# Attention and two gated MLPs on one core: the second pass's products with w_in, w_gate and w_val by a Strassen scheme

## The chip, the cores and the metric

The kernel runs on one core of one Trainium2 chip. The metric is the device time of one execution in microseconds, the median of three runs. PE (TensorE) multiplies, DVE (VectorE), ACT (ScalarE) and POOL (GpSimd) work elementwise, and all transfers are issued from the queue of SP (SyncE).

## What is computed

```python
scores = cap * np.tanh(scale * q @ k^T / cap)        # batch 4, 12 heads, 448 tokens, head size 64
attn   = softmax(scores) @ v                         # -> x, 1792 tokens x 768
x = np.maximum(x @ w_in, 0) ** 2 @ w_out             # 768 -> 2048 -> 768
y = (sigmoid(x @ w_gate) * (x @ w_val)) @ w_out2     # 768 -> 1536 -> 768
```

The weights come as 64-bit floats.

## The kernel before

The tokens are worked off in two passes. The first pass has 768 tokens, as column blocks of 256 and 512; the second has 1024, as two blocks of 512. Each pass runs both MLPs. Attention comes first and then runs interleaved with the first pass, since x of the second pass is needed late. The feature dimension of 768 is six tiles of 128 (`CC`); the hidden layers are 16 and 12 tiles, taken in groups of four (`FG`).

Every float32 product is made of three: each operand is split into a rounded high half (`hi`, by ACT) and the rest (`lo = x - hi`, by DVE for activations, by POOL for weights), and `products` adds lo·hi, hi·lo and hi·hi into one PSUM bank (lines 540 to 542). A unit is one such product: with w_in, w_gate or w_val it has 6 x 3 matmuls (`unit_a`), with an output matrix 4 x 3 (`unit_b`). Four banks, tag `pn`, go round; a bank is free again when its result has been taken out: by ACT for the relu (`relu`) and the sigmoid (`gate`), by DVE for the gate's product (`val`, line 585) and for the additions into `acc` (`total`, line 603). After that the hidden values are split again (`split_g`, tiles `gx`).

In the first pass each weight tile is converted from 64 bits on DVE (lines 498 to 504, tile `raw`), kept in DRAM in 32 bits, split (`round_w`, tiles `wh` and `wl`, four of each) and used; the second pass loads the 32-bit copy and splits it again. x of the second pass is split as soon as it is ready, stored to DRAM (`xn`, `store_x`), and loaded again once attention is through (`load_x`), into tiles `xa` in memory that attention has left. Between the passes the pool `mlp0` is closed and `mlp1` opened in its place (`turn_over`).

The order of each engine's instructions is written when the program is built: `Flow` plays the jobs off against costs per operation (lines 131 to 150), each engine takes what is ready by rank and age, and `pick` gives PE the next unit or attention step. On the chip each engine then works in that fixed order and waits on semaphores.

## Time and profile before

| | |
|---|---|
| median of 3 runs | 1204.4 us (1204.39 to 1205.56) |
| span of the profiled execution | 1206.0 us |
| PE busy | 1182.8 us (98%), 5880 matmuls |
| DVE, ACT, POOL busy | 661.7 (55%), 583.5 (48%), 277.0 us (23%) |
| mean granted TensorE clock | 0.995 |

The profiled execution has no time of its own beside its span, so the span stands for it; it is 1.6 us above the median of the runs. Busy time of PE counts matmuls from their start to their modelled end, so overlapping ones fill it up. All times of an engine are from the trace of this one execution.

### The profile page before, as it was taken

Reading aid. Unit: us, or ns where it says so; the run is one execution under the profiler, and the core shown is the slowest. Engines: PE = TensorE matmul, PEld = TensorE weight load, DVE = VectorE, ACT = ScalarE, POOL = GpSimd, SP = SyncE. Lnnn points to the kernel's source line nnn. Section 1 sums busy time; section 2 is a strip of 40 time slices with the busy share of each in tenths; the row PEclk is TensorE's granted clock in tenths of the full one; section 3 lists DMA queues with packets and bytes.
Section 4 is the critical chain, followed back from the end, with each engine's and each line's share of the span. In section 5 each row is a group of like instructions: output and inputs, shape, how many; then the busy total and the mean of one; then the engine's idle time right before and its main releaser. Section 6 shows DMA issues by size and latency. Waiting matters only on the chain.

```text
span 1206.0 us, 15410 instructions
## 1 busy us (share of the span) xinstructions
PE 1182.8 (98%) x5880; PEld 968.0 (80%) x5880; DVE 661.7 (55%) x943; ACT 583.5 (48%) x862; POOL 277.0 (23%) x174
## 2 busy tenths in 40 slices
PE   7999999998999989999999999999999999999998
PEld 4556788887888878888888888888888888888887
DVE  3699789888989988889972102212153210221222
ACT  7876567574677677765533434251432223221220
POOL 0021222322212223222322221312122123123110
PEclk9999999999999999999999999999999999999999
DMA  4565666555645656555686111211121112112112
GB/s 161 151 196 153 183 195 181 189 170 164 187 143 175 191 164 211 179 184 176 177 287 228 40 58 35 70 28 60 45 61 53 35 44 66 40 40 66 44 44 96
DMA packets 70490, 149.81 MB, mean 124 GB/s; under 512 B 20497, under 2 KB 28945, under 8 KB 70417
## 3 DMA queue, kind: packets, MB, share of 16 engines
q1 hardware_dynamic: 70416, 148.84, 40.0%
q8 instruction: 46, 0.75, 0.2%
q14 instruction: 28, 0.22, 0.1%
HBM read 110.10 MB, written 38.62 MB: 123 GB/s over the span
## 4 chain that ended last, share of the span: by engine, by line
PE 80%; DVE 11%; DMA 3%; ACT 3%; issue 2%; SPq 0%; POOL 0%; DVEq 0%; ACTq 0%; POOLq 0%
PE pn L540 24%; PE pn L541 24%; PE pn L542 24%; PE pv L365 6%; PE se L321 2%; DVE raw L502 2%; DVE raw L504 1%; DVE raw L500 1%; ACT pt L212 1%; DVE raw L498 1%; DVE pt L408 1%; DVE pt L215 1%; DMA sg<-pt 1%; DMA s_wv<-raw 1%; DMA w<-in_w_dram 1%
## 5 line engine op out<-in xcount | busy, mean ns | idle before, releaser
L525 POOL TENSOR_TENSOR wl<-raw,wh 128x512 fp32r<-128x512 f32 (+1 forms) x164 | 274.0, 1671 | 897.5 <-ACT wh L212 739.7
L540 PE MATMUL pn<-xa,wl 128*128 128x512 f32 (+1 forms) x960 | 350.2, 365 | 0.0
L541 PE MATMUL pn<-xa,wh 128*128 128x512 f32 (+1 forms) x960 | 349.6, 364 | 0.0
L542 PE MATMUL pn<-xa,wh 128*128 128x512 f32 (+1 forms) x960 | 349.1, 364 | 0.0
L212 ACT ACTIVATE wh<-raw 128x512 fp32r<-128x512 f32 (+1 forms) x160 | 117.2, 732 | 313.1 <-PE pn L542 259.8
L541 PE MATMUL pn<-gx,wh 128*128 128x512 f32 (+1 forms) x672 | 244.3, 364 | 3.9 <-DVE gx L215 3.9
L540 PE MATMUL pn<-gx,wl 128*128 128x512 f32 (+1 forms) x672 | 244.6, 364 | 0.0
L542 PE MATMUL pn<-gx,wh 128*128 128x512 f32 (+1 forms) x672 | 244.0, 363 | 0.0
L540 PEld LDWEIGHTS pn<-xa,wl 128*128 128x128 f32 x960 | 182.1, 190 | 31.2 <-issue 3.0
L542 PEld LDWEIGHTS pn<-xa,wh 128*128 128x128 f32 x960 | 182.1, 190 | 28.5
L541 PEld LDWEIGHTS pn<-xa,wh 128*128 128x128 f32 x960 | 182.0, 190 | 27.9
L215 DVE TENSOR_TENSOR gx<-g,gx 128x512 fp32r<-128x512 f32 (+1 forms) x112 | 87.1, 778 | 161.4 <-ACT gx L212 160.9
L541 PEld LDWEIGHTS pn<-gx,wh 128*128 128x128 f32 x672 | 127.1, 189 | 23.6 <-DVE gx L215 4.3
L603 DVE TENSOR_TENSOR acc<-pn,acc 128x512 f32<-128x512 f32 (+1 forms) x120 | 74.3, 621 | 127.4 <-PE pn L542 126.8
L540 PEld LDWEIGHTS pn<-gx,wl 128*128 128x128 f32 x672 | 127.0, 189 | 21.4 <-issue 1.9
L542 PEld LDWEIGHTS pn<-gx,wh 128*128 128x128 f32 x672 | 127.1, 189 | 19.8
L585 DVE TENSOR_TENSOR g<-pn,r 128x512 f32<-128x512 f32 (+1 forms) x48 | 29.7, 620 | 169.7 <-PE pn L542 169.7
L365 PE MATMUL pv<-pt,v 128*128 128x448 f32 x360 | 112.7, 447 | 5.2 <-DVE pt L218 1.9
L365 PEld LDWEIGHTS pv<-pt,v 128*128 128x128 f32 x360 | 64.6, 189 | 39.5 <-issue 23.0
L212 ACT ACTIVATE gx<-g 128x512 fp32r<-128x512 f32 (+1 forms) x112 | 64.5, 576 | 64.6 <-DVE g L585 62.6
L212 ACT ACTIVATE r<-pn 128x512 f32<-128x512 f32 (+1 forms) x112 | 59.8, 534 | 66.8 <-PE pn L542 66.7
L212 ACT ACTIVATE raw<-w 128x512 f32<-128x512 f32 (+1 forms) x78 | 60.9, 781 | 57.3 <-DMA s_w<-raw 21.1
(71 smaller groups left out, 1044.8 us busy)
## 6 DMA issues: line engine op xcount, KB each, us to landing
w<-in_w_dram SPq DMA_DIRECT2D x16, 768.0 KB
w<-in_w_dram SPq DMA_DIRECT2D x24, 512.0 KB
w<-in_wg_dram SPq DMA_DIRECT2D x12, 768.0 KB
w<-in_wv_dram SPq DMA_DIRECT2D x12, 768.0 KB
w<-in_wo_dram SPq DMA_DIRECT2D x18, 512.0 KB
s_w<-raw SPq DMA_DIRECT2D x16, 384.0 KB
s_w<-raw SPq DMA_DIRECT2D x24, 256.0 KB
xa<-xn SPq DMA_DIRECT2D x12, 512.0 KB
```

What stands on the lines that cost most here:

```text
L212: return on("ACT", flow.act(cols(out)) + extra, lambda: nc.scalar.activation(out=out, in_=in_, func=func, **kw), rank)
L215: return on("DVE", flow.dve(cols(out)), lambda: nc.vector.tensor_tensor(out=out, in0=a, in1=b, op=ALU.subtract), rank)
L321: nc.tensor.matmul(out=sc[:, x, :S], lhsT=w[r, c0:c0 + P], rhs=a[r, :S], start=i == 0, stop=i == 2)
L365: nc.tensor.matmul(out=o[:, j, :S], lhsT=w, rhs=pt[r, u], start=step == 0 and m == 0, stop=step == 3 and m == len(terms) - 1)
L408: yield on("DVE", flow.dve(S), lambda: nc.vector.tensor_tensor(out=xu[r], in0=xe[r, j], in1=bc[r], op=ALU.mult), 0 if early(n) else 2)
L502: yield on("DVE", flow.dve(n), lambda: nc.vector.scalar_tensor_tensor(out=mu, in0=lo, scalar=29, in1=mu, op0=ALU.logical_shift_right, op1= ...
L525: yield on("POOL", 0.15 + n * 0.0023, lambda: nc.gpsimd.tensor_tensor(out=lo, in0=raw, in1=f32(hi), op=ALU.subtract))
L540: nc.tensor.matmul(out=o, lhsT=wl[:, s], rhs=hi, start=i == 0, stop=False)
L541: nc.tensor.matmul(out=o, lhsT=wh[:, s], rhs=lo, start=False, stop=False)
L542: nc.tensor.matmul(out=o, lhsT=wh[:, s], rhs=hi, start=False, stop=i == n - 1)
L585: yield on("DVE", flow.dvep(w), lambda: nc.vector.tensor_tensor(out=g, in0=o, in1=st["r", k, f, off], op=ALU.mult))
L603: yield on("DVE", flow.dvep(w), lambda: nc.vector.tensor_tensor(out=acc, in0=o, in1=acc, op=ALU.add))
```

## The change

Only the second pass changes its products with w_in, w_gate and w_val. Two hidden tiles of 128 (f and f + 2) by two blocks of 512 tokens are one group: the weights are blocks a11, a12, a21, a22 (hidden tile by half of the six feature tiles), the activations b11, b12, b21, b22 (half of the feature tiles by token block). Four outputs took eight block products of 3 x 3 matmuls; now seven take their place, numbered 1 to 7:

- sums of weights, DVE, 384 columns each: s1 = a21 + a22, s2 = s1 - a11, s3 = a11 - a21, s4 = a12 - s2
- differences of activations, DVE, 512 columns each: t1 = b12 - b11, t2 = b22 - t1, t4 = t2 - b21, t3 = b22 - b12
- products: 1 = a11·b11, 2 = a12·b21, 3 = s4·b22, 4 = a22·t4, 5 = s1·t1, 6 = s2·t2, 7 = s3·t3
- PE takes them as 1, 2, 6, 4, 7, 5, then product 1 of the next group, then 3. Products 1, 6 and 7 are added up in one bank, each copied out by ACT between (`cp`); 5 and 3 share another bank. DVE makes the outputs: 2 + cp1, 4 subtracted from cp7, 5 + cp7 and 3 + cp6.

All sums are of float32 before the split into high and low halves, which now is made for 7 x 3 activation tiles (before 6 of double width) and, per group, for 7 weight halves of 384 columns. There are 8 groups for w_in and 12 for w_gate and w_val.

Around it: x of the second pass is stored unsplit (half the bytes), loaded in 12 pieces of 256 KB and combined (`combine`); for the second MLP `second` combines the sums of w_out. Four more banks, tag `pq`, take the place that attention's banks leave. The closing products with w_out and the last matrix start with the hidden tiles of the first group (units of 6 matmuls, `part`). The weights of the second pass go through the two `w64` tiles. Early q and k tiles use the buffers of `gx`.

```diff
-WSTART, ATT, XGAP, SLACK = 5, 0.82, 2.0, 1.0
+WSTART, ATT, SLACK = 5, 0.82, 1.0
+R1, G1, CP, TM = 8, 3, 5, 3
+HK = CC // 2
+RANK = {"x": 1, "y": 0}
+FORM = {"1": "b11", "2": "b21", "6": "t2", "4": "t4", "7": "t3", "5": "t1", "3": "b22"}
...
+    def after_attention():
+        close_pool("att")
+        close_pool("ps")
+        open_pool("act1", "right")
...
+        open_pool("units1", "left", space=bass.MemoryType.PSUM)
...
+    def split(kind, name, i, src, temp=None):
...
+        yield act(dst[:, 0], src, rank=RANK[kind])
+        yield sub(dst[:, 1], src, f32(dst[:, 0]), RANK[kind])
...
+    def combine(kind, i, raw, event):
...
+        yield sub(t1, raw["b12"], raw["b11"], RANK[kind])
...
+        yield sub(t2, raw["b22"], t1, RANK[kind])
...
+        yield sub(t4, t2, raw["b21"], RANK[kind])
...
+        yield sub(t3, raw["b22"], raw["b12"], RANK[kind])
...
+    def weight_sums(grp, raw):
...
+        yield add2(s1, a21, a22)
+        yield sub(s2, s1, a11)
...
+        yield sub(s3, a11, a21)
+        yield sub(s4, a12, s2)
...
+    def low(m, h, hi, lo, src, res, item):
+        n = cols(src)
+        yield on("POOL", 0.15 + n * 0.0023, lambda: nc.gpsimd.tensor_tensor(out=lo, in0=src, in1=f32(hi), op=ALU.subtract))
...
+    def strassen(u, kind, gi, j, num):
+        grp = kind, gi, j
+        m, h = u["m"], u["half"]
+        slot = ("bank", grp, {"1": "b", "6": "b", "7": "b", "2": "a", "4": "d", "5": "e", "3": "e"}[num])
...
+        o = products(m, HK, lambda i: st[src, FORM[num], i], 0, SP, st[slot], h * HW, first=bool(u["bank"]))
+        return shares(grp, num, o)
+
+    def shares(grp, num, o):
...
+        if num in "167":
+            yield "take", "cp"
+            t = st["cp", grp, num] = T("mlp1", "cp", [P, SP], bufs=CP)
+            yield act(t, o, rank=0)
...
+        part = {"2": "1", "4": "7", "5": "7", "3": "6"}[num]
+        yield "until", ("cp", grp, part)
+        yield "take", "r1"
+        c = T("mlp1", "r", [P, SP], bufs=R1)
+        yield post(c, o, st["cp", grp, part], ALU.subtract if num == "4" else ALU.add)
...
+        needs += {"6": [("cp", grp, "1")], "7": [("cp", grp, "6")], "3": [("sum", grp, "5")]}.get(num, [])
...
+                    for num in "126475":
+                        add_s(kind, gi, j, num)
+                        if held and num == "1":
+                            add_s(*held, "3")
```

Where the instructions move, on DVE: the end of the first pass, from the low half of the last hidden tile (`gx`) on; `acc` rows give PE its banks back, `raw` rows convert weights. Before:

```order
L215 TENSOR_TENSOR gx<-g,gx 128x512
L498 TENSOR_SCALAR raw<-raw 128x512
L603 TENSOR_TENSOR acc<-pn,acc 128x256
L500 TENSOR_SCALAR raw<-raw 128x512
L502 SCALAR_TENSOR_TENSOR raw<-w_6281,raw 128x512
L504 SCALAR_TENSOR_TENSOR raw<-w_6281,raw 128x512
L603 TENSOR_TENSOR acc<-pn,acc 128x512 x2
```

Changed, from the same row on (`tm` is a difference, `xa` a low half):

```order
L220 TENSOR_TENSOR gx<-g,gx 128x512
L220 TENSOR_TENSOR xa<-tm,xa 128x512
L822 TENSOR_TENSOR acc<-pn,acc 128x256
L220 TENSOR_TENSOR tm<-tm,xa 128x512
L647 TENSOR_SCALAR raw<-raw 128x512
L649 TENSOR_SCALAR raw<-raw 128x512
L822 TENSOR_TENSOR acc<-pn,acc 128x256
L220 TENSOR_TENSOR xa<-xa 128x512
L220 TENSOR_TENSOR xa<-tm,xa 128x512
L220 TENSOR_TENSOR tm<-xa,tm 128x512
```

Rows of the second pass's x now stand between the additions.

On DVE, the end of the second pass's products with w_out. Before, additions and low halves alternate:

```order
L603 TENSOR_TENSOR acc<-pn,acc 128x512
L215 TENSOR_TENSOR xa<-acc,xa 128x512
L603 TENSOR_TENSOR acc<-pn,acc 128x512
L215 TENSOR_TENSOR xa<-acc,xa 128x512
L603 TENSOR_TENSOR acc<-pn,acc 128x512
L215 TENSOR_TENSOR xa<-acc,xa 128x512
L585 TENSOR_TENSOR g<-pn,r 128x512
```

Changed, up to the addition for product 2 of the first w_gate group (`r<-cp,pq`):

```order
L822 TENSOR_TENSOR acc<-pq,acc 128x512
L822 TENSOR_TENSOR acc<-pn,acc 128x512
L822 TENSOR_TENSOR acc<-pq,acc 128x512
L220 TENSOR_TENSOR tm<-acc 128x512
L220 TENSOR_TENSOR xa<-acc,xa 128x512
L220 TENSOR_TENSOR tm<-acc,tm 128x512
L220 TENSOR_TENSOR xa<-acc,xa 128x512
L220 TENSOR_TENSOR xa<-tm,xa 128x512
L220 TENSOR_TENSOR tm<-tm,acc 128x512
L220 TENSOR_TENSOR xa<-tm,xa 128x512
L226 TENSOR_TENSOR r<-cp,pq 128x512
```

The last three additions now come in one piece, and seven rows of the last operands follow.

On PE, the first group of w_in, from the last matmul of product 2 to the first of product 4, with what each row waits for:

```order
L698 MATMUL pq<-xa,wh 128x512
L695 MATMUL pn<-xa,wl 128x512 [waits Activation_49,Pool_49]
L697 MATMUL pn<-xa,wh 128x512
L698 MATMUL pn<-xa,wh 128x512
L695 MATMUL pn<-xa,wl 128x512
L697 MATMUL pn<-xa,wh 128x512
L698 MATMUL pn<-xa,wh 128x512
L695 MATMUL pn<-xa,wl 128x512
L697 MATMUL pn<-xa,wh 128x512
L698 MATMUL pn<-xa,wh 128x512
L695 MATMUL pq<-xa,wl 128x512 [waits Pool_49]
```

Before, a unit was 18 such rows in a bank of its own; product 6 here goes on in the bank of product 1, behind ACT's copy.

## Rows read from the trace of the kernel before

**Rows 1.** The page: busy us, share of the span and instructions of each engine.
```profile
PE 1182.8 (98%) x5880; PEld 968.0 (80%) x5880; DVE 661.7 (55%) x943; ACT 583.5 (48%) x862; POOL 277.0 (23%) x174
```

**Rows 2.** Windows: length, busy us of PE, PEld, DVE, ACT, POOL, clock, DMA, GB/s.
```profile
648.00:1200.00 552.00, 552.00 (x2437) 457.24 (x2436) 119.27 (x152) 163.54 (x259) 122.49 (x79) 1.00 0.17 52
600.00:650.00 50.00, 50.00 (x281) 43.88 (x280) 29.51 (x47) 15.19 (x25) 14.75 (x11) 1.00 0.89 311
```

**Rows 3.** Timeline: start, us, engine, line; 256 columns, the second pass's start, its end.
```profile
591.22 0.28 PE L542 MATMUL pn<-xa,wh 128*128 128x256 f32 x1
...
591.34 0.28 PE L540 MATMUL pn<-xa,wl 128*128 128x256 f32 x1
...
647.31 0.39 PE L540 MATMUL pn<-xa,wl 128*128 128x512 f32 x1
...
1201.96 0.39 PE L542 MATMUL pn<-gx,wh 128*128 128x512 f32 x1
```

**Rows 4.** Timeline of DVE, end of the first pass; in brackets the idle time before.
```profile
614.66 0.69 DVE L215 TENSOR_TENSOR gx<-g,gx 128x512 fp32r<-128x512 f32 x1 [0.70 <-ACT gx L212]
615.73 0.43 DVE L498 TENSOR_SCALAR raw<-raw 128x512 f32<-128x512 f32 x1 [0.38 <-ACT raw L212]
...
620.66 0.69 DVE L502 SCALAR_TENSOR_TENSOR raw<-w,raw 128x512 uint32<-128x512 uint32 x1
...
640.60 0.42 DVE L603 TENSOR_TENSOR acc<-pn,acc 128x256 f32<-128x256 f32 x1 [0.74 <-PE pn L542]
...
647.51 0.69 DVE L603 TENSOR_TENSOR acc<-pn,acc 128x512 f32<-128x512 f32 x1 [2.03 <-PE pn L542]
```

**Rows 5.** Groups by form from 640 us on: xcount | busy us, mean ns | idle, releaser.
```profile
L525 POOL TENSOR_TENSOR wl<-raw,wh 128x768 fp32r<-128x768 f32 x39 | 71.8, 1842 | 173.8 <-ACT wh L212 173.8
...
L525 POOL TENSOR_TENSOR wl<-raw,wh 128x512 fp32r<-128x512 f32 x42 | 54.3, 1294 | 243.1 <-ACT wh L212 243.1
L215 DVE TENSOR_TENSOR gx<-g,gx 128x512 fp32r<-128x512 f32 x56 | 49.3, 880 | 153.9 <-ACT gx L212 153.9
L603 DVE TENSOR_TENSOR acc<-pn,acc 128x512 f32<-128x512 f32 x62 | 42.9, 691 | 108.5 <-PE pn L542 108.0
...
L212 ACT ACTIVATE wh<-raw 128x768 fp32r<-128x768 f32 x39 | 33.0, 847 | 117.0 <-PE pn L542 108.7 <-DMA raw<-s_w 5.6 <-issue 2.7
L212 ACT ACTIVATE r<-pn 128x512 f32<-128x512 f32 x56 | 32.9, 588 | 62.5 <-PE pn L542 62.5
L212 ACT ACTIVATE wh<-raw 128x512 fp32r<-128x512 f32 x42 | 26.6, 633 | 116.1 <-PE pn L542 112.9 <-POOL wl L525 3.2
```

**Rows 6.** Timelines of DVE, then POOL; last, the window of rows 4.
```profile
587.22 2.20 DVE L500 TENSOR_SCALAR raw<-raw 128x768 uint32<-128x768 uint32 x1
...
593.14 0.54 DVE L500 TENSOR_SCALAR raw<-raw 128x768 uint32<-128x768 uint32 x1
...
587.15 1.85 POOL L525 TENSOR_TENSOR wl<-raw,wh 128x768 fp32r<-128x768 f32 x1 [5.08 <-ACT wh L212]
...
615.70:648.20 32.50, 32.50 (x187) 28.68 (x186) 16.23 (x28) 7.97 (x12) 10.91 (x7) 1.00 0.98 362
```

**Rows 7.** Timelines of SP's queue, then ACT: x stored, reloaded; first eviction.
```profile
607.33 0.58 SPq L222 DMA_DIRECT2D xn<-pt  x1
...
614.40 1.29 SPq L455 DMA_DIRECT2D xa<-xn  x2
...
651.59 0.60 ACT L212 ACTIVATE r<-pn 128x512 f32<-128x512 f32 x1 [1.81 <-PE pn L542]
```

**Rows 8.** Timeline of PE at two gaps, then windows of 5 us around them.
```profile
279.17 0.39 PE L541 MATMUL pn<-gx,wh 128*128 128x256 f32 x1 [3.27 <-DVE gx L215]
...
586.17 0.68 PE L365 MATMUL pv<-th,v 64*128 64x448 f32 x4 [0.93 <-DVE th L215]
...
280.00:285.00 5.00, 5.00 (x24) 4.06 (x23) 3.82 (x8) 1.68 (x2) 0.00 (x0) 0.66 0.84 220
...
590.00:595.00 5.00, 5.00 (x33) 4.47 (x32) 4.37 (x8) 2.17 (x4) 1.64 (x1) 1.00 0.58 162
```

More of the change, by code (lines that the diff above doesn't have):

```diff
@@ L316, in scores @@
         turn = (n + step) % 3
-        sc = bank2("so" if turn == 0 else "si", open_pools["more"][1]) if early(n) and turn < 2 else bank2("se")
+        sc = bank2("so" if turn == 0 else "si", "more") if early(n) and turn < 2 else bank2("se")
         c0 = S + step * P
@@ L461, in source @@
+    scratch, left, loads, plan, groups = {}, {}, [], [], []
     def source(key):
@@ L530, in round_w, with bank, products @@
         flow.put("raw")
-    def products(m, n, operand, off, w):
+    def bank(resource):
+        pool, tag = ("units", "pn") if resource == "pn" else ("units1", "pq")
+        return open_pools[pool][1].tile([P, 512], F32, tag=tag, name=tag, bufs=4)
+    def products(m, n, operand, off, w, o=None, begin=0, end=None, first=True):
         wh, wl = st["w", m]
-        o = open_pools["units"][1].tile([P, 512], F32, tag="pn", name="pn", bufs=4)[:, :w]
-        for i in range(n):
-            s = slice(i * P, (i + 1) * P)
+        o = bank("pn")[:, :w] if o is None else o
+        chain = not first
+        for i in range(n) if end is None else end:
+            s = slice(begin + i * P, begin + (i + 1) * P)
@@ L559, in relu, with square @@
         flow.put("pn")
+        yield from square(k, off, w, f, r)
+    def square(k, off, w, f, r):
         yield "take", f"g{k}"
[L561 removed]
+        g = T(f"mlp{k}", "g", [P, SP], bufs=G1 if k else 2)[:, :w]
         yield act(g, r, AF.Square)
@@ new lines, in attn_mlp_kernel, with add @@
+    blocks = PASSES[0][1]
+    def add(tiles, kind, i, blk, fn, *args):
+        off, w = blk
+        if kind == "w1":
+            needs = [("x", 0, p, x) for p in range(NP) for x in ([S, T0] if off else [S])]
+        elif kind in ("wg", "wv"):
+            needs = [("y", 0, c, off) for c in range(CC)]
+        else:
+            needs = [("g", 0, i[0] * FG + f + (F1 if kind == "wo" else 0), off) for f in range(FG)]
+        key = (0, kind, i)
+        if key not in keys:
+            keys.append(key)
+        m = keys.index(key)
+        units.append({"us": us(w, 3 * tiles), "m": m, "key": key, "needs": needs + [("w", m)], "fn": fn,
+            "bank": "pn", "back": "pn", "args": (kind, 0, *blk, *args)})
@@ new lines, in attn_mlp_kernel, with add_s @@
+    n0 = len(units)
+    def add_s(kind, gi, j, num):
+        src = "x" if kind == "w1" else "y"
+        grp = kind, gi, j
+        if grp not in loads:
+            loads.append(grp)
+            groups.append(grp)
+        if pairing and len(plan[pairing[-1]]) == 1:
+            m, h = pairing[-1], 1
+        else:
+            m, h = len(plan), 0
+            pairing.append(m)
+            plan.append([])
+        plan[m].append((grp, num))
+        needs = [(src, FORM[num], i) for i in range(HK)] + [("w", len(keys) + m, h)]
+        needs += {"6": [("cp", grp, "1")], "7": [("cp", grp, "6")], "3": [("sum", grp, "5")]}.get(num, [])
+        units.append({"us": us(SP, 3 * HK), "m": len(keys) + m, "half": h, "key": (1, kind, (gi, j)), "needs": needs,
+            "fn": strassen, "bank": {"1": "pn", "5": "pn", "2": "pq", "4": "pq"}.get(num), "args": (kind, gi, j, num)})
```

379 lines of the change are left out of this document (276 added, 103 removed).

## The prediction

> **What bounds the kernel now.** The page comes first: PE is busy 98% of the span [rows 1]. A busy PE need not be a PE at its limit, so the windows come next: from 648 to 1200 us PE is busy all 552 us, while DVE, ACT and POOL are each busy under a third of them, and the clock is 1.00, the upper of its two levels (2.4 GHz) [rows 2]. The matmuls in order of time then give the pace: the second pass starts at 647.31 and its last matmul at 1201.96 [rows 3]; 2448 matmuls of 512 columns lie there, so (1201.96 - 647.31) / 2447 = 0.2267 us each, without a gap. The second pass costs its number of matmuls times 0.2267 us, and any microsecond for which PE now has to wait there is new. The first pass is another stage: DVE is busy 29.5 us of 50 even at its end [rows 2], and PE does wait for DVE there [rows 8]. The traced span is 1206.0 us; the median of the three runs, 1204.4, is 1.6 us less. The sum is made against the span and 1.6 us are then taken off. About 0.2% (2.4 us) is what a measurement can tell from no change.
>
> **Term 1, the products.** PE's order holds 5604 matmuls for 5784. The 180 that go are all of the second pass and of 512 columns: 1440 matmuls with w_in, w_gate and w_val become 7/8 of that, 1260. PE never waits in that stretch, so they count in full: 180 x 0.2267 = **-40.8 us**. LDWEIGHTS go with them.
>
> **Term 2, the end of the first pass.** Each of the three pairs of x tiles now needs 11 rows on DVE (4 differences, 7 low halves), 33 in all, and in the changed order they stand among the last 30 old rows of the first pass, ahead of the additions that give banks back. At their own length: 33 x 0.69 = 22.8; six additions at 0.42 and six at 0.69, 6.7; two gate products and two gx rows, 2.2; twelve conversion rows, 3 x (0.43 + 0.43 + 0.69 + 0.69) = 6.7; two weight sums of 384 columns at 0.69 x 384/512 = 0.52, 1.0: together 39.4 us [rows 4, 5]. Before, the same old rows ran from 615.73 to 648.20, 32.5 us [rows 4]. DVE is thus 6.9 us too long for the stretch. Three things shift this. POOL's low halves: a DVE row that reads only SBUF waits while POOL runs (0.54 us is its own length; 2.20 us it took beside a POOL row of 1.85) [rows 6], and POOL has seven rows, 10.9 us, in this stretch [rows 6]. The stretch may start earlier: the last attention product is now followed by 18 more matmuls of 512 and 36 more of 256 columns than before, 18 x 0.2267 + 36 x 0.12 = 8.4 us [rows 3], and x is stored without its split, from 607.33 before and first reloaded at 614.40 [rows 7]. And PE may lead the additions by four banks: the last product needs only the addition four before its own. After that one DVE has 5.4 us of rows; the product itself is 2.7 (12 matmuls), and before, the last addition ended 0.9 behind it, so 5.4 - 2.7 - 0.9 = 1.8 us are free. Lower end 6.9 - 8.4 - 1.8, that is 0; upper end 6.9 + 10.9 - 1.8 = 16.0. With half of POOL's time and half of the earlier start: 6.9 + 5.5 - 4.2 - 1.8 = 6.4. I take **+6**, nearer the lower end, because the gx row of the same form lasts 0.69 when POOL lets it and 0.88 on average [rows 4, 5].
>
> The Trainium skill (SBUF — State Buffer, section "SBUF: two separate sides") says more: DVE and GpSimd share a port pair under an exclusive lock for whole instructions. By it a full DVE pays all of POOL's time, and this term would be 16 instead of 6, term 4 would be 6 instead of 3, and the sum some 13 us higher. The 2.20 us row agrees; that additions out of PSUM keep 0.69 [rows 5] shows that not every row is hit.
>
> **Term 3, the pools' turn.** The first product's copy goes to ACT into memory of the first pass, so it waits for the last output store; product "6" writes the same bank and waits for the copy. Products "1" and "2" hide 18 x 0.2267 = 4.1 us. Before, the last addition ended at 648.20 [rows 4] and the first eviction into this memory started at 651.59, right behind its matmul [rows 7], so issue and landing of the store took at most 3.4 us. Addition 0.69, store up to 3.4, copy 0.59 [rows 5], the matmul's tail 0.16 (0.39 less the pace): 4.8 at most. 0 to 0.7; I take **+0.5**.
>
> **Term 4, between w_out and w_gate.** The y operands need the same 33 rows. From the first closing addition of w_out's last group to the low half that product "6" reads last, DVE has 45 rows: 12 additions, 30 y rows, 3 weight sums, 42 x 0.69 + 3 x 0.52 = 30.5 us [rows 5]. PE has in the same stretch 3 x 6 + 8 x 12 + 2 x 9 + 6 = 138 matmuls, 31.3 us. POOL's six rows there (two at 1.29, four at an estimated 1.01, on the line through 1.29 at 512 and 1.84 at 768 columns [rows 5]) add 0 to 6.6. So 0 to 5.8; half of POOL gives 2.5, and I take **+3**.
>
> **Term 5, handovers in 20 groups.** "6" waits for ACT's copy of "1", "7" for that of "6", "3" for DVE's addition to "5". Each has another product, 9 x 0.2267 = 2.04 us, between. A copy is 0.59 plus the matmul's tail of 0.16: 1.3 us are left, more than any ACT row of this stage (0.63). An addition can stand behind one DVE row that POOL holds: 1.01 + 0.69, then its own 0.69 and 0.16, 2.55 us, 0.5 too many; 20 x 0.5 = 10. Bounds 0 and 10; POOL is busy 7 x 1.01 of 14.3 us in a group, half, and the held row must stand just there, so **+3**.
>
> **Term 6, the clock.** After PE stood still for 3.27 us, the next 5 us ran at a granted 0.66, that is partly at 1.2 GHz: 5 x 0.34 = 1.7 us; a gap of 0.93 us left it at 1.00 [rows 8]. One long gap, at term 2, is likely: **+1.5**, bounds 0 and 4.
>
> **Term 7, attention.** DVE loses 18 subtractions and ACT 12 copies of x there, and early q and k tiles come from other buffers. PE is full in most of that stage, but a stall like that of 3.27 us plus its 1.7 can vanish or appear: **0**, bounds -5 and +5.
>
> Costed at nothing: POOL's work grows from 39 x 1.84 + 42 x 1.29 = 126 us to some 140 x 1.01 + 42 x 1.29 = 196 of 514 [rows 5], with four weight tiles ahead of PE; weights move the same bytes, and x half of them; SP's issues stay near their number. The last addition and store, from 1201.96 to the end, stay as they are.
>
> Sum: 1206.0 - 40.8 + 6 + 0.5 + 3 + 3 + 1.5 + 0 = 1179.2 of span, less 1.6 = 1177.6; **forecast 1178 us**, own range 1170 to 1188.
>
> **The rivals.**
> *All hidden.* The lower ends of terms 2 to 6 come true: 1204.4 - 40.8 = 1163.6, up to 1169. For it: DVE's lower sum fits at both changes of operand. Against: 39.4 us of rows where 32.5 were.
> *DVE and POOL set the pace.* Upper ends: 16.0 + 0.7 + 5.8 + 10 + 4 = 36.5, so 1206.0 - 40.8 + 36.5 - 1.6 = 1200; from 1188 on, middle 1194. For it: in a pair of w_gate and w_val groups DVE has 4 x 0.69 (additions) + 4 x 3 x 0.69 (addition, product, low half) + 8 x 0.52 (weight sums) = 15.2 us and POOL 14 x 1.01 = 14.1, together 29.3 against PE's 126 x 0.2267 = 28.6. Against: eight of those rows read PSUM and pass POOL by.
> *Slower: the bank that three products share.* "1", "6" and "7" go through one bank, PE's order is fixed, so a late copy stops everything. 60 handovers; from 40.8 / 60 = 0.68 us of wait each the gain is gone, at 1 us each and nothing else the time is 1224. For it: in a w_in group ACT has 4 x (0.59 + 0.63 + 0.63) + 3 x 0.59 + 7 x 0.52 = 12.8 of 14.3 us to do [rows 5] (0.52 for a split of 384 columns, on the line through 0.63 at 512 and 0.85 at 768). Against: the 1.3 us left above. The Trainium skill (TensorE: Matmul & The Clock Gate, section "A second HAM failure mode: psum-queue depth-cycling") tells of a kernel whose pauses between groups, as it went round its PSUM banks, kept switching its clock. Here that is the same mechanism with term 6 on top, and no row of the second pass shows a clock under 1.00.
> *No change.* The removed matmuls were hidden anyway: 1204. Against: the pace above.
>
> **How the numbers follow.** Forecast 0.55, all hidden 0.20, DVE and POOL 0.16, slower 0.06, no change 0.03. The first three are faster by over 0.2%: 0.91; same 0.03; slower 0.06. The range reaches from all hidden to the middle of the third case: 1164 to 1195.
>
> **What would show it.** The second pass with 2268 matmuls at 0.2267 us, some 514 us. Waits of PE on DVE or ACT of 5 to 8 us around the end of the first pass, of 2 to 4 at the first w_gate product, and short ones at "3". Term 2 is wrong if PE has no gap between the last attention product and the second pass. Many waits on ACT copies of over 0.5 us, or a clock below 1.00 across the second pass, would make the prediction wrong.

## The result, and the profile after

The changed kernel takes 1175.5 us (median of 4 runs, 1173.6 to 1178.7), the kernel before 1204.4 in the same session (1200.7 to 1205.6): a ratio of 0.977, 95% interval 0.975 to 0.980. The forecast was 1178 us, range 1164 to 1195. The profiled execution took 1173.6 us, 1171.9 of it in the trace.

The page's line of the changed kernel, to be read beside [rows 1]:

```profile
PE 1142.3 (97%) x5700; PEld 932.7 (80%) x5700; DVE 792.0 (68%) x1133; ACT 658.9 (56%) x1044; POOL 362.6 (31%) x274
```

Its windows answer to [rows 2]: the second pass, the 50 us around the end of the first, and 5 us of those.

```profile
652.00:1167.00 515.00, 513.66 (x2262) 423.77 (x2261) 242.03 (x331) 230.31 (x427) 205.40 (x179) 1.00 0.17 55
600.00:650.00 50.00, 45.50 (x249) 39.95 (x248) 47.68 (x79) 22.63 (x41) 12.21 (x9) 0.93 0.65 221
625.00:630.00 5.00, 5.00 (x19) 4.61 (x20) 5.00 (x10) 3.02 (x6) 0.00 (x0) 0.50 0.15 59
```

DVE, ACT and POOL have each become busier in the second pass (DVE from 22% to 47% of the time, POOL from 22% to 40%), and PE is still busy all but 1.3 of 515 us. From 600 us on, DVE is full in two places. One is the end of the first pass (47.7 of 50 us), and there alone the clock is off its upper level: 0.50 is 1.2 GHz for all of that window, right behind a gap of 3.59 us. The other is the change from w_out to w_gate, where the operands of the second MLP are made:

```profile
875.00:905.00 30.00, 29.69 (x131) 24.14 (x129) 29.96 (x45) 15.78 (x28) 8.65 (x6) 1.00 0.15 53
```

The timeline of PE: the first and the last matmul of the second pass, as in [rows 3], and between them its two only waits of over 0.1 us.

```profile
651.33 0.39 PE L695 MATMUL pn<-xa,wl 128*128 128x512 f32 x1
...
902.47 0.50 PE L697 MATMUL pn<-xa,wh 128*128 128x512 f32 x1 [0.31 <-DVE xa L220]
...
906.31 0.50 PE L695 MATMUL pn<-xa,wl 128*128 128x512 f32 x1 [1.03 <-POOL wl L629]
...
1167.86 0.39 PE L698 MATMUL pq<-gx,wh 128*128 128x512 f32 x1
```

From 651.33 to 1167.86 lie 2268 matmuls, 516.53 us; before it were 554.65 [rows 3]. 2267 x 0.2267 is 513.9, so 2.6 us are not pace: 0.47 and 1.19 at the two waits, 0.3 in the slower matmuls behind them, 0.6 in four places where a matmul or two start late without idle time in the record (term 5 below says what they are).

PE's timeline at the end of the first pass:

```profile
619.84 0.28 PE L698 MATMUL pn<-gx,wh 128*128 128x256 f32 x1
621.03 0.38 PE L695 MATMUL pn<-gx,wl 128*128 128x256 f32 x1 [0.91 <-ACT gx L217]
625.00 0.58 PE L697 MATMUL pn<-gx,wh 128*128 128x256 f32 x1 [3.59 <-DVE gx L220]
...
628.16 0.63 PE L695 MATMUL pn<-gx,wl 128*128 128x512 f32 x1
```

From 619.84 to 625.00, two matmuls of 256 columns take 5.16 us instead of 0.24: 4.9 us of waiting. Up to 630.56 the matmuls stand 0.21 (256 columns) and 0.43 us (512) apart, half speed: 1.5 us lost over fourteen of them and 1.0 over six, 2.5 us together. What PE waits for is seen on DVE:

```profile
616.00 1.79 DVE L220 TENSOR_TENSOR xa<-tm,xa 128x512 fp32r<-128x512 f32 x1
...
620.12 0.41 DVE L795 TENSOR_TENSOR g<-pn,r 128x256 f32<-128x256 f32 x1
620.45 0.67 DVE L220 TENSOR_TENSOR xa<-tm,xa 128x512 fp32r<-128x512 f32 x1
621.05 0.68 DVE L653 SCALAR_TENSOR_TENSOR raw<-w,raw 128x512 uint32<-128x512 uint32 x1
621.65 0.68 DVE L220 TENSOR_TENSOR tm<-xa 128x512 f32<-128x512 f32 x1
622.26 0.68 DVE L220 TENSOR_TENSOR xa<-xa 128x512 fp32r<-128x512 f32 x1
622.86 0.68 DVE L220 TENSOR_TENSOR xa<-tm,xa 128x512 fp32r<-128x512 f32 x1
623.46 0.68 DVE L795 TENSOR_TENSOR g<-pn,r 128x512 f32<-128x512 f32 x1
624.06 0.89 DVE L220 TENSOR_TENSOR gx<-g,gx 128x256 fp32r<-128x256 f32 x1
```

The gate product g of 256 columns had its inputs at 615, when the last matmul into its bank ended. It starts at 620.12, behind five x rows and a row of a conversion; its low half gx starts at 624.06, behind four more x rows, another row of the conversion and a second g. Beside a POOL row (615.86 to 617.24), the x row of 616.00 lasts 1.79 us. Rows of 512 columns last 0.68 us by the record but stand 0.60 apart when the queue is full.

**Where the time went.** The last attention product starts at 574.7 us, before at 586.5, 11.8 us earlier; 8.4 of these are only work that now stands behind it (term 2). From there to the second pass are 76.6 us instead of 60.8: 8.4 of moved work and 7.4 of cost. The second pass is 38.1 us shorter, the tail from its last matmul is 4.0 us in both. -11.8 + 15.8 - 38.1 = -34.1, the difference of the two spans. Of the first term 3.4 us are left that no part of the change explains; the first experiment is about them.

### The profile page after: what moved, and what is told of

Read it like the earlier page. It is cut to its first block, busy times and chain, and to the rows that moved or that the text cites. A ratio compares the mean times of both kernels' runs of the same rounds, so it can differ in the third digit from the quotient of the medians.

```text
span 1171.9 us, 15590 instructions
## 1 busy us (share of the span) xinstructions
PE 1142.3 (97%) x5700; PEld 932.7 (80%) x5700; DVE 792.0 (68%) x1133; ACT 658.9 (56%) x1044; POOL 362.6 (31%) x274
## 4 chain that ended last, share of the span: by engine, by line
PE 72%; DVE 14%; ACT 7%; DMA 4%; issue 3%; SPq 0%; POOL 0%; ACTq 0%; DVEq 0%
PE pn L695 16%; PE pn L697 16%; PE pn L698 15%; PE pv L376 7%; PE pq L695 5%; PE pq L698 5%; PE pq L697 5%; PE se L332 2%; DVE raw L651 2%; ACT L217 2%; DVE raw L653 2%; DVE xa L220 2%; ACT pt L217 2%; DVE raw L647 1%; ACT raw L217 1%
## 5 line engine op out<-in xcount | busy, mean ns | idle before, releaser
L674 POOL TENSOR_TENSOR wl<-raw,wh 128x512 fp32r<-128x512 f32 (+1 forms) x82 | 150.5, 1835 | 482.2 <-ACT wh L217 331.8
L695 PE MATMUL pn<-xa,wl 128*128 128x512 f32 (+1 forms) x780 | 279.4, 358 | 1.0 <-POOL wl L629 1.0
L697 PE MATMUL pn<-xa,wh 128*128 128x512 f32 (+1 forms) x780 | 278.5, 357 | 0.3 <-DVE xa L220 0.3
L698 PE MATMUL pn<-xa,wh 128*128 128x512 f32 (+1 forms) x780 | 278.1, 357 | 0.0
L629 POOL TENSOR_TENSOR wl<-w,wh 128x384 fp32r<-128x384 f32 (+1 forms) x102 | 125.3, 1232 | 207.7 <-ACT wh L217 207.3
L697 PE MATMUL pn<-gx,wh 128*128 128x512 f32 (+1 forms) x504 | 179.8, 357 | 6.2 <-DVE gx L220 6.2
L695 PE MATMUL pn<-gx,wl 128*128 128x512 f32 (+1 forms) x504 | 180.1, 357 | 0.9 <-ACT gx L217 0.9
L698 PE MATMUL pn<-gx,wh 128*128 128x512 f32 (+1 forms) x504 | 179.1, 355 | 0.0
L217 ACT ACTIVATE wh<-raw 128x384 fp32r<-128x384 f32 (+2 forms) x158 | 97.3, 621 | 144.6 <-PE pn L698 61.7
L697 PEld LDWEIGHTS pn<-xa,wh 128*128 128x128 f32 x780 | 147.4, 189 | 21.6 <-DVE xa L220 0.7
L698 PEld LDWEIGHTS pn<-xa,wh 128*128 128x128 f32 x780 | 147.2, 189 | 21.3
L629 POOL TENSOR_TENSOR wl<-raw,wh 128x384 fp32r<-128x384 f32 x80 | 86.1, 1086 | 88.1 <-ACT wh L217 88.1
L697 PEld LDWEIGHTS pn<-gx,wh 128*128 128x128 f32 x504 | 96.2, 191 | 19.4 <-DVE gx L220 6.6
L698 PEld LDWEIGHTS pn<-gx,wh 128*128 128x128 f32 x504 | 96.2, 191 | 13.4
L217 ACT ACTIVATE raw<-w 128x512 f32<-128x512 f32 (+1 forms) x78 | 60.8, 780 | 65.6 <-DMA s_wg<-raw 20.4
```

The lines of the kernel that those rows point to most:

```text
L217: return on("ACT", flow.act(cols(out)) + extra, lambda: nc.scalar.activation(out=out, in_=in_, func=func, **kw), rank)
L629: yield on("POOL", 0.15 + n * 0.0023, lambda: nc.gpsimd.tensor_tensor(out=lo, in0=src, in1=f32(hi), op=ALU.subtract))
L674: yield on("POOL", 0.15 + n * 0.0023, lambda: nc.gpsimd.tensor_tensor(out=lo, in0=raw, in1=f32(hi), op=ALU.subtract))
L695: nc.tensor.matmul(out=o, lhsT=wl[:, s], rhs=hi, start=first, stop=chain, skip_group_check=chain)
L697: nc.tensor.matmul(out=o, lhsT=wh[:, s], rhs=lo, start=False, stop=chain, skip_group_check=chain)
L698: nc.tensor.matmul(out=o, lhsT=wh[:, s], rhs=hi, start=False, stop=chain or stop, skip_group_check=chain)
```

## The experiments

Ratios are to the kernel before, run on the same chip in the same session.

### The kernel before, once more: what is chance in term 7

No edit.

> The kernel before, unchanged, profiled a second time, for term 7 and the clock. If the clock lost after PE's gaps near 122, 276 and 427 us (1.7 us each, 5.1 in all, in the first profile) belongs to the kernel, all three drops are there again and the last attention product lies within 1 us of 586.5. If it is chance, as the profiles of the changed kernel's variants suggest (0 to 5.2 us lost in the same stretch, behind the same gaps), the number of drops differs or may differ, and the product's place moves by 1.7 us with each drop. The second pass takes 554.7 us either way.

It took 1201.3 us, 1199.2 of span. The window from 120 to 130 us, of this run and of two others (columns as in [rows 2]; the clock is the third from the right):

```profile
120.00:130.00 10.00, 8.59 (x41) 6.62 (x38) 9.21 (x20) 5.17 (x9) 1.46 (x1) 1.00 0.75 223
```

The changed kernel:

```profile
120.00:130.00 10.00, 7.86 (x37) 6.10 (x34) 8.01 (x16) 4.62 (x8) 0.91 (x1) 1.00 0.59 177
```

The variant with one rank changed far behind this place (below):

```profile
120.00:130.00 10.00, 7.86 (x30) 5.89 (x29) 8.77 (x17) 3.75 (x5) 0.00 (x0) 0.83 0.64 187
```

In the first profile of the kernel before, three stretches behind gaps (at 125, 280 and 430 us) had a clock of 0.66, 1.7 us each; [rows 8] show one of them. Here none has, and the last attention product starts at 579.7 instead of 586.5. The other two fences show one order of instructions and the same 7.86 us of busy PE in 10, once at a clock of 1.00 and once at 0.83. Over all profiles of the changed kernel and of its variants the attention part lost between 0 and 5.1 us in this way. So a profile's own time carries a chance of 5 us, and the 3.4 us that the attention part seemed to gain are of this kind. Like for like, neither losing any, it is 579.7 - 8.4 = 571.3 against 574.7: by these two profiles attention is 3.4 us slower, 2.9 of it in small waits (20.1 us of idle PE up to 585 us, here 17.2). The kernel before alone differs by 1.4 us between its two profiles (18.6 and 17.2), so how much of this belongs to the change is not shown. From the last attention product to the second pass it is 60.8 us again, and the second pass takes 554.65 us to the hundredth.

### The eighth product put back

```diff
+        if num == "2":
+            products(m, HK, lambda i: st[src, FORM[num], i], 0, SP, st[slot], h * HW)
         o = products(m, HK, ...)
...
-        units.append({"us": us(SP, 3 * HK), ...
+        units.append({"us": us(SP, (6 if num == "2" else 3) * HK), ...
```

Product 2 of every group is run twice, and the second line tells the planner so.

> Edit: product "2" of every group is run twice into its bank (the second run starts the sum anew), 20 x 9 = 180 more matmuls of 512 columns; nothing else is added, and every other row stays. Term 1 (the pace sets the second pass): 180 x 0.2267 = 40.8 us more than the changed kernel's span of 1171.9, less at most the 1.7 us of waits near 902 to 906 us that the longer groups may cover: span 1211 to 1213, that is 5 to 7 us over the kernel before, because all other terms stay paid. Rival, the removed matmuls were hidden anyway: no more than 3 us over the changed kernel. Rival, DVE and POOL set the pace: well under 40.8 us more, since the added matmuls would fill waits.

1216.9 us, ratio 1.013 (1.011 to 1.015). The second pass, first and last matmul:

```profile
654.95 0.39 PE L695 MATMUL pn<-xa,wl 128*128 128x512 f32 x1
...
1210.62 0.39 PE L698 MATMUL pq<-gx,wh 128*128 128x512 f32 x1
```

555.67 us for 2448 matmuls: 39.1 more than in the changed kernel, that is 40.8 less the 1.7 of waits that the longer groups now cover. The ratios say the same: 0.0354 of 1203 is 43 us, and the intervals leave 37 to 48. Term 1 holds, and the removed matmuls were not hidden. With eight products, everything else that the change brings costs 1.3%: the gain is the one product of eight that is left out, and nothing else.

### Rows of x behind all others

```diff
-RANK = {"x": 1, "y": 0}
+RANK = {"x": 2, "y": 0}
```

> Edit: one number; the rows that make the x operands go behind every other row that is ready on ACT and DVE (rank 2 for 1). No row is added or left out, and the matmuls' order is the same. Theory A (order): the wait of 0.91 + 3.59 us at the first closing product of the first pass stands there because the gate product on DVE, its copy and its low half are queued behind some ten x rows; here they run first, the wait goes, with it the half speed of the clock after it (2.5 us), and the second pass starts about 7 us earlier, near 644: time 1165 to 1168 on a chip where the changed kernel takes 1173.6. Theory B (the sum, as term 2 had it): DVE has more rows than the stretch holds, so the wait comes back later, at the first products with the differences ("6", "4", "7" of the first group): time within 2 us of the changed kernel's.

1180.0 us, ratio 0.982 (0.980 to 0.983). The wait at gx is down to 0.4 us and the second pass starts 70.0 us behind the last attention product. But there, PE waits for x:

```profile
654.92 0.80 PE L697 MATMUL pn<-xa,wh 128*128 128x512 f32 x1 [3.98 <-DVE xa L220]
...
661.14 0.51 PE L697 MATMUL pq<-xa,wh 128*128 128x512 f32 x1 [2.01 <-DVE xa L220]
```

Its second pass takes 524.8 us, 8.3 more: these two waits, and behind them the clock falls again. Theory B had the place right, the wait comes back; its time (within 2 us) is missed, since by the ratios this order is 5 us slower.

### Gate rows first in the last group

```diff
-                out=g, in0=o, in1=st["r", k, f, off], op=ALU.mult))
+                out=g, in0=o, in1=st["r", k, f, off], op=ALU.mult), 0 if f == F2 - 1 else 1)
...
-        yield act(dst[:, 0], g)
-        yield sub(dst[:, 1], g, f32(dst[:, 0]))
+        first = 0 if (k, f) == (0, F1 + F2 - 1) else 1
+        yield act(dst[:, 0], g, rank=first); yield sub(dst[:, 1], g, f32(dst[:, 0]), first)
```

> Edit: in the first pass's last group alone the gate product, its copy and its low half go ahead of the x rows that are ready (four rows of rank 0 for 1); nothing else is ranked anew, the matmuls' order is the same. With DVE full from 615 to 650 us the x rows then end later in relation to PE, but the product that reads the last of them ("7", the fifth of its group) started some 10 us after that row's end, so there is room. Theory A' (the wait was in the wrong place; 10 us of room lay unused behind it): the 4.5 us and the 2.5 us of half clock go, new waits under 2 us: time 5 to 7 us less than the changed kernel's 1175.5, 1168 to 1171. Theory B (the sum): the wait moves behind, to the last tiles of w_out, whose weights DVE now converts later, or to "6", "4" and "7": time within 2 us of the changed kernel's.

1181.3 us, ratio 0.981 (0.979 to 0.983): worse than either theory had it. No wait at gx, but PE's timeline, then DVE's and POOL's, show what is late now:

```profile
649.92 0.58 PE L695 MATMUL pn<-gx,wl 128*128 128x256 f32 x1 [10.20 <-POOL wl L674]
```
```profile
643.25 0.68 DVE L653 SCALAR_TENSOR_TENSOR raw<-w,raw 128x512 uint32<-128x512 uint32 x1
```
```profile
644.80 5.07 POOL L674 TENSOR_TENSOR wl<-raw,wh 128x512 fp32r<-128x512 f32 x1 [14.58 <-ACT wh L217]
```

The wait bears POOL's name, and POOL had been idle for 14.6 us. What starts late is DVE's: the last step of a weight tile's conversion (643.25) stands behind x rows; ACT's copy and POOL's low half follow it. Then this low half lasts 5.07 us, where the next one, at 649.83, lasts 1.27. DVE's rows follow each other without a gap up to 648.75, and POOL's ends 1.1 us behind them: as the rows stand, a full DVE held POOL, and some 3.8 of the 10.2 us are that.

### Gate rows and conversions first

```diff
-        yield on("DVE", flow.dve1(n), ...)
+        yield on("DVE", flow.dve1(n), ..., 0 if m >= len(keys) - 2 else 1)
```

This is done in the four DVE rows and the two ACT rows of a conversion, on top of the edit before.

> Edit: in the last group of the first pass the gate product, its copy and its low half, and the conversion of the last two weight tiles (four rows on DVE, two on ACT for each), go ahead of the x rows that are ready; the weight sums stay behind them. No row is added or left out, the matmuls' order is the same. The orders tried so far left the wait at gx (4.5 us), at the x operands (6.0 us, x rows last of all) or at a weight tile (10.2 us, conversions behind the x rows). If the wait is a matter of which row is late, this one has the three kinds of rows in the order in which PE needs them, DVE's last x rows end some 36 us after the stretch begins, within 1 to 2 us of their products, and 4 to 6 us are gained: 1169 to 1172, ratio to the kernel before 0.971 to 0.974. If DVE's sum decides alone, any order pays 4 us or more: 1175 to 1181.

1179.2 us, ratio 0.980 (0.978 to 0.983). Now additions and the first copy of the second pass are late:

```profile
636.05 0.50 PE L695 MATMUL pn<-gx,wl 128*128 128x512 f32 x1 [3.12 <-DVE acc L822]
...
658.06 0.56 PE L695 MATMUL pn<-xa,wl 128*128 128x512 f32 x1 [3.86 <-ACT cp L217]
```

The second wait is term 3's. Here the first copy starts only at 657.32, 3.76 us behind the start of the last addition (653.56), as its memory comes free with the store of that; in the changed kernel it was 2.86 us, and hidden. The time lies in the range given for the case that any order pays (1175 to 1181).

### Fewer rows on DVE: the differences left out

```diff
-        yield sub(t1, raw["b12"], raw["b11"], RANK[kind])
+        t1 = raw["b12"] if late else (yield sub(t1, raw["b12"], raw["b11"], RANK[kind])) or t1
```

The same is done for t2 (b22), t4 (b21) and t3 (b11). The kernel leaves the twelve differences out, so its second pass multiplies other operands.

> Left out: the twelve differences of x tiles on DVE (their low halves and copies are made from plain x tiles instead, so the second pass multiplies other operands); 8.2 us of DVE rows less at the end of the first pass, matmuls' order the same. About as many rows as before still stand ahead of the gate product and of gx there. Theory B (the sum of DVE's rows, term 2): 39.4 - 8.2 = 31.2 us fit into the stretch, so the wait of 4.5 us at the first closing product goes and the second pass starts 5 to 8 us after what the attention part gives less. Theory A (order alone: what stands ahead of gx): the wait stays at 3 to 4.5 us, since the number of rows ahead of gx hardly changes, and only what comes after it is freed.

1175.6 us (one run), and the wait is still there: 1.3 us, then 4.2.

```profile
622.33 0.39 PE L695 MATMUL pn<-gx,wl 128*128 128x256 f32 x1 [1.31 <-ACT gx L217]
626.90 0.58 PE L697 MATMUL pn<-gx,wh 128*128 128x256 f32 x1 [4.19 <-DVE gx L220]
```

Twelve rows less and no gain: as theory A said, as many rows stand ahead of gx as before. Then both edits at once:

> Both edits together: the twelve differences of x tiles are left out (8.2 us of DVE rows less; the second pass multiplies other operands), and the gate product, its copy and its low half go first in the last group. Each alone moved or kept the wait (5.5 us at gx with the rows left out; 3.3 us at gx gone but 10.2 us at a weight tile with the new order). If DVE's sum in this stretch is what PE pays for, and the order only says where, then with both no wait over 1 us is left from 600 us to the end of the first pass, the clock stays at 1.00 there, and from the last attention product to the first product of the second pass it is 69 to 71 us instead of 76.6. If conversion of weights is late for another reason, a wait of 3 us or more stays at a low half made by POOL.

1176.9 us (one run); waits of 1.25 us at a gx and of 2.51 at a weight tile, the clock at half once; 75.2 us from the last attention product to the second pass, not 69 to 71. Less than with either edit alone, but not gone. So neither theory is right by itself, and the table puts them together. It gives, from one trace each, what each order pays at the change of pass: the time from the last attention product to the second pass above 69.2 us (60.8 + 8.4, no wait), and that of the second pass above 516.5.

| kernel | before the second pass | in it | sum |
|---|---|---|---|
| changed kernel | 7.4 | 0 | 7.4 |
| x rows last | 0.8 | 8.3 | 9.1 |
| gate rows first | 11.8 | 0 | 11.8 |
| gate rows and conversions first | 4.3 | 5.5 | 9.8 |
| differences left out | 8.7 | 0 | 8.7 |
| left out, and gate rows first | 6.0 | 0 | 6.0 |
| differences on POOL, gate rows first (below) | 18.9 | 0 | 18.9 |

How far one trace can be trusted: five runs below and above (the eighth product, low halves on DVE, POOL at one and a half, 6 before 7, y in turn) leave this stretch as it is but for a few rows at its end, and pay 6.8 to 8.6 us before the second pass. So 8.7 with the differences left out is no change, and 6.0 is at most a small gain on 7.4. DVE's queue is full for 35 us: which row is late is a matter of order, and none of three other orders of the same rows was cheaper than the planner's; here they cost 2 to 4 us more, by the ratios 3 to 5 (the interval of x rows last only touches the changed kernel's, the other two overlap it). That the rows themselves cost shows with gate rows first: there the same twelve rows less take 11.8 to 6.0. Whether 8.2 us fewer rows with conversions first would clear the wait was not tried.

### The differences on POOL

```diff
-        yield sub(t1, raw["b12"], raw["b11"], RANK[kind])
+        yield diff(t1, raw["b12"], raw["b11"])
```

Here diff gives POOL the subtraction for x, for all four differences, on top of gate rows first.

> Edit: the twelve differences of x tiles are made by POOL (1.3 us each, 15.6 us) instead of DVE (8.2 us), and the gate product, its copy and its low half go first in the last group; nothing is left out. POOL was idle from 624.7 to 639.3 and has some 11 us of weight tiles in this stretch. If POOL's rows cost DVE little (the seven of them there stretched DVE's by some 3.7 us in all, 0.5 each), DVE gains 8.2 and loses about 6, so most of the wait stays: 1174 to 1178. If they run beside each other, the wait and the half clock behind it go: 1168 to 1171. If the low halves of the weights queue behind the differences on POOL, a wait of 2 to 5 us comes at a weight tile: 1178 to 1182.

1186.7 us, ratio 0.985 (0.982 to 0.988): the dearest order, and over all three forecasts. Window, DVE and POOL, and the wait:

```profile
615.00:655.00 40.00, 28.02 (x143) 23.48 (x141) 38.97 (x48) 17.84 (x32) 20.79 (x16) 0.92 0.43 156
```
```profile
620.09 1.78 DVE L220 TENSOR_TENSOR xa<-xa 128x512 fp32r<-128x512 f32 x1
```
```profile
619.96 1.36 POOL L489 TENSOR_TENSOR tm<-tm,xa 128x512 f32<-128x512 f32 x1
```
```profile
656.49 0.58 PE L700 MATMUL pn<-gx,wl 128*128 128x256 f32 x1 [8.62 <-POOL wl L679]
```

POOL is busy 20.8 us and DVE, with twelve rows less, is still busy 39 of 40. A DVE row that meets a POOL row lasts up to 1.78 us instead of 0.68. In this window thirteen rows of DVE are 12.9 us longer than their own length, more than the 8.2 us that went to POOL: they came back as waiting.

### Low halves of the weights on DVE

```diff
-        yield on("POOL", 0.15 + n * 0.0023, lambda: nc.gpsimd.tensor_tensor(out=lo, in0=src, in1=f32(hi), op=ALU.subtract))
+        yield sub(lo, src, f32(hi))
```

> Edit: in the second pass the low halves of the weights are made by DVE instead of POOL (181 rows); POOL does nothing after the first pass. Matmuls' order the same. My account: a pair of w_gate and w_val groups gives DVE 15.2 + 14 x 0.52 = 22.5 us of PE's 28.6, every row at its own length since no POOL row holds it; no wait of PE but at the change of operands, where DVE gets six rows of 0.5 to 0.7 more in a stretch that was full (waits there 3 to 5 us instead of 1.3): time 0 to 5 us over the changed kernel. Rival, DVE and POOL set the pace through the lock between them: without POOL the waits go and the time falls by 2 us or more. DVE rows of the form gx<-g,gx 128x512, 900 ns on average from 650 us on in the changed kernel, fall to about 690 ns if POOL is what holds them; they stay at 900 if it is not.

1178.3 us, ratio 0.980 (0.977 to 0.982). DVE's groups by form, without POOL:

```profile
L220 DVE TENSOR_TENSOR gx<-g,gx 128x512 fp32r<-128x512 f32 x56 | 38.0, 690 | 18.9 <-ACT gx L217 18.6
...
L226 DVE TENSOR_TENSOR r<-cp,pn 128x512 f32<-128x512 f32 x40 | 27.5, 688 | 32.1 <-PE pn L698 31.3
```

and in the changed kernel, beside POOL:

```profile
L220 DVE TENSOR_TENSOR gx<-g,gx 128x512 fp32r<-128x512 f32 x56 | 49.5, 900 | 34.1 <-ACT gx L217 33.8
...
L226 DVE TENSOR_TENSOR r<-cp,pn 128x512 f32<-128x512 f32 x40 | 27.4, 684 | 34.5 <-PE pn L698 33.5
```

900 ns become 690: it is POOL that holds rows which read only SBUF; the sums that read PSUM keep 684 to 688. The second pass takes 516.3 us, as before. The lock exists, and there it costs PE nothing that can be told (516.5 with it).

### POOL at one and a half

```diff
-        ... nc.gpsimd.tensor_tensor(out=lo, in0=src, in1=f32(hi), op=ALU.subtract))
+        ... [nc.gpsimd.tensor_tensor(out=lo[:, :k], in0=src[:, :k], in1=f32(hi)[:, :k], op=ALU.subtract) for k in (n // 2, n)])
```

> Edit: in the second pass POOL makes the first half of each low half of the weights twice (181 rows of half the columns more); POOL's work there grows from about 208 to some 310 us of 516, DVE's rows and the matmuls' order stay. My account: POOL and DVE hold each other up (DVE's gx rows 900 ns beside POOL, 690 without it), but both have idle time: the waits of PE grow by 1 to 4 us, mostly at the change of operands, where a weight tile comes later: time 1176 to 1181 where the changed kernel takes 1175.5. Rival, DVE and POOL set the pace: a pair of w_gate and w_val groups then has 22.4 us of POOL and 15.2 us of DVE, 37.6 together against PE's 28.6; if even the 10 us of DVE rows that read only SBUF count, 6 pairs lose 4 us each and more: 24 us or more over the changed kernel.

1184.4 us, ratio 0.984 (0.982 to 0.986), against 0.977. The second pass takes 523.7 us, 7.1 more, and its two costliest waits (us, times, longest) are these:

```profile
PE pn L695 <- DVE r L226: 3.0, 3, 1.6
PE pn L695 <- POOL wl L629: 1.7, 1, 1.7
```

The three waits on r are term 5's: "3" waits for the addition to "5". In two of them the additions stand behind a weight sum that POOL held (1.36 us for 0.54); before the third, DVE itself had waited for ACT's copy. So my account was too low (1 to 4 us) and the rival much too high (24); with POOL at 40% these handovers cost 0.6 us in all (term 5 below), at 65% they begin to bite.

### A handover without cover

```diff
-                    for num in "126475":
+                    for num in "126745":
```

> Edit: PE's order of the seven products is 1 2 6 7 4 5 3 instead of 1 2 6 4 7 5 3, so "7" follows "6" directly into the same bank, with no product between to hide ACT's copy of "6"; 20 such handovers, no row added or left out. Term 5's account: each then waits for the whole copy, 0.59 + 0.16 for the matmul's tail, some 0.75 to 0.9 us: 20 waits, 15 to 18 us in all; with the clock staying at 1.00 (none of them is over 1 us) the time is 1190 to 1194 where the changed kernel takes 1175.5. Rival, the pauses switch the clock: granted clock well below 1.00 over the stages of w_in, w_gate and w_val, and each pause costs up to 1.7 us more, 1200 to 1228. Rival, ACT is so busy in these stages that the copy stands behind two other ACT rows: waits of 1.5 to 2 us each, 1206 to 1216, which would say that the handovers were near their limit all along.

1200.4 us, ratio 0.998 (0.996 to 0.999): nearly the whole gain is gone. One handover in PE's timeline, the waits of the second pass (us, times, longest), and windows on either side of the first w_gate group:

```profile
964.72 0.39 PE L698 MATMUL pn<-xa,wh 128*128 128x512 f32 x1
965.88 0.47 PE L695 MATMUL pn<-xa,wl 128*128 128x512 f32 x1 [0.78 <-ACT cp L217]
```
```profile
PE pn L695 <- ACT cp L217: 14.1, 16, 1.2
PE pn L695 <- POOL wl L629: 5.4, 4, 2.9
```
```profile
655.00:900.00 245.00, 238.40 (x1043) 194.98 (x1043) 100.37 (x142) 123.74 (x221) 93.86 (x80) 1.00 0.17 53
920.00:1195.00 275.00, 265.03 (x1151) 215.13 (x1151) 120.80 (x162) 98.63 (x186) 107.67 (x96) 1.00 0.17 56
```

From 964.72 to 965.88 is 1.16 us, 0.93 over the pace. The second pass takes 541.1 us, 24.6 more; 1.9 of it is the wait on POOL at the first w_gate group, 2.9 us here and 1.03 in the changed kernel, and 1.7 the clock behind that. That wait is the handover of this group. The other 21 us are the handovers of the other 19 groups, at 1.1 us. (Three of them bear POOL's name in the waits, where its low half ended last.) The time is that of the rival in which the pauses switch the clock, but the clock stays at 1.00 over 245 and 275 us with these pauses in them. The mechanism was right, the price too low: 0.59 + 0.16 for the copy is not all, in the handover shown going from PE to ACT and back adds some 0.2.

### Rows of y in turn with the weight sums

```diff
-RANK = {"x": 1, "y": 0}
+RANK = {"x": 1, "y": 1}
```

> Edit: one number; the rows that make the y operands lose their precedence over the weight sums (rank 1 for 0), at the change from w_out to w_gate. Matmuls' order the same. Theory A: the 1.03 us that PE waits for POOL's low half at 906 us is DVE's: the weight sum that this low half needs was queued behind the last y rows (it ran at 904.14). With the sums in turn, that wait goes, and the wait on y rows (0.31 us now) grows to about 1 us: waits of PE from 890 to 920 us 0.5 to 1.5 us in all, time within 1 us of the changed kernel's. Theory B: POOL itself is short of time there: the wait on it stays at about 1 us.

1183.7 us (one run), outside both theories. The wait on POOL is gone, and in its place stand two on the y operands:

```profile
908.86 0.50 PE L695 MATMUL pn<-xa,wl 128*128 128x512 f32 x1 [4.15 <-ACT xa L217]
911.28 0.79 PE L697 MATMUL pn<-xa,wh 128*128 128x512 f32 x1 [1.91 <-DVE xa L220]
```

4.15 and 1.91 us for 1.03 and 0.31, and the clock behind them falls to half. That the low half was late through DVE's sum holds (DVE's row at 904.14, POOL's at 905.26, below), that the exchange would be even does not.

```profile
904.14 0.55 DVE L220 TENSOR_TENSOR raw<-w,raw 128x384 f32<-128x384 f32 x1
```
```profile
905.26 0.99 POOL L629 TENSOR_TENSOR wl<-raw,wh 128x384 fp32r<-128x384 f32 x1 [13.48 <-ACT wh L217]
```

## Why the prediction was right, term by term

| term | forecast | measured |
|---|---|---|
| 1, products | -40.8 | -40.8 (180 fewer, 0.2267 us each; the eighth product put back gave 39.1) |
| 2, end of the first pass | +6 | +4.9 |
| 6, clock | +1.5 | +2.5 |
| 3, pools' turn | +0.5 | 0 |
| 4, y operands | +3 | +2.0 (0.47 + 1.19, and 0.3 behind them) |
| 5, handovers | +3 | +0.6, at four of 20 |
| 7, attention | 0 | -3.4 against the first profile, +3.4 against the second |

Terms 2 to 6 were to cost 14.0 us and cost 10.0. With term 7 left out the span would have come 4.0 us under the forecast; that attention too came out lower, by 3.4, comes of the chance that the second profile of the kernel before shows.

**Terms 1 and 3** hold by their own steps. **Term 4** holds in its mechanism: DVE has no gap of over 0.1 us from 872 to 905, and the late row is a weight sum behind the y rows, a row of the kind that the term counted. Its sizes met by luck. The rows stand closer than their length (see term 2), and five of them, beside POOL, lasted 4.0 us over their own length, where 3.3 was taken.

**Term 2** came out near, but two of its steps failed. It let PE wait for the additions that give banks back. That is not what stops PE: it is the gate product and gx, rows that the sum counted as 2.2 us of work, and not as rows that PE waits for and that each stand behind six others. And the lengths: rows of 0.69 stand 0.60 apart in a full queue, so 39.4 us of rows are some 34 (33 x 0.60 = 19.8; additions 6 x 0.34 + 6 x 0.60 = 5.6; gate rows 1.9; conversions 3 x (0.34 + 0.34 + 0.60 + 0.60) = 5.6; sums 0.9). POOL adds less than the 5.5 us, half of its time, that I took: the rows of DVE that its rows held (1.79, 1.52, 1.36 and three shorter ones) lasted 3.9 us over their own length. 34 + 3.9 are 5 us more than 32.5, and the 4.2 us of earlier start that I set against it were not to be had, since the late row stands at the beginning of the stretch. Errors of both signs met, and that the term came out near is luck.

**Term 5** was sized at 3 for a held row at "3". It occurs in four of the 20 groups, at 665, 926, 1016 and 1106 us, and costs some 0.15 us each time. DVE's row before the addition and the addition to "5", then the first matmul of "3":

```profile
1104.66 1.37 DVE L746 TENSOR_TENSOR g<-r 128x512 f32<-128x512 f32 x1
1105.96 0.67 DVE L226 TENSOR_TENSOR r<-cp,pn 128x512 f32<-128x512 f32 x1
```
```profile
1106.78 0.47 PE L695 MATMUL pn<-xa,wl 128*128 128x512 f32 x1
```

The row of 1104.66 lasts 1.37 us beside a POOL row (1104.47 to 1105.49), and "3" starts 0.15 us behind the addition's end at 1106.63. The profile counts no idle time there, as the matmul before is recorded up to 1106.88. At the other three places "3" starts as far behind its addition, and rows of 1.36 or 1.37 us stand ahead of it; with POOL at one and a half, where the profile does name DVE, the lag is 0.15 us too (935.82 and 935.97). So the mechanism was right and its size was not: the held row lasts 1.37 us, not 1.70, and PE waited in four groups. With POOL's work at one and a half PE waited at "3" three times, 3.0 us.

**Term 6**: the gap was the one expected, the loss 2.5 us instead of 1.7.

**Term 7** was left at 0 with 5 us to either side, and that is what it needs: the clock after gaps in attention moves a run by up to 5.1 us, before and after alike. The sum against the second profile of the kernel before closes too: 1199.2 + 3.4 + 7.4 - 38.1 = 1171.9.

**The rivals.** All hidden: 7.4 us at the change of pass and 2.0 at w_gate are not. DVE and POOL set the pace: the lock is there (900 and 690 ns), but in the second pass DVE is busy 47%, and PE's waits for the two are 1.3 us by the record, at the first w_gate group; at the end of the first pass, where DVE is full, it is real, as the differences on POOL show. The rule of the Trainium skill (SBUF — State Buffer, section "SBUF: two separate sides") of an exclusive lock between DVE and GpSimd agrees with the rows of 1.78 us and with the 690 ns without POOL. What the forecast drew from it, that a full DVE pays all of POOL's time, does not: from 615.7 to 651.2 us POOL is busy 9.4 us (seven rows), and DVE's rows are 3.9 longer than their own. The bank shared by three products: with a product between, no handover waits for ACT's copy; without it 1.1 us each, so 60 of them would cost 66 by that estimate, more than the gain. The Trainium skill's tale of a clock that switches as PSUM banks are cycled (TensorE: Matmul & The Clock Gate, section "A second HAM failure mode: psum-queue depth-cycling") is not what these 19 pauses, most of them 0.78 us of idle PE, did: 1.00 in the windows above. No change: the eighth product excludes it.

## What to carry to other kernels

Where PE had no gap, matmuls removed counted in full, at the pace of the trace; the price of the scheme lies where its operands are made, at the change of pass, and there the question is not only how many rows the vector engine gets but which row PE waits for, and how deep it stands in the queue. Before a rank is changed to free one row, list the rows that it passes: three other orders here were no cheaper than the one planned. A product placed between two that share a bank was worth 1 us per handover. And a start later than the pace can be a wait where the profile counts no idle time.
